# A written-out list of operations in place of a greedy scheduler, with GpSimd conversions, work in halves and means copied by engines

## The chip, the cores and the metric

The kernel runs on one core of one Trainium2 chip. The core has five engines with queues of their own, each of which works strictly in order: TensorE (PE in the rows; PEld is its weight load), VectorE (DVE), ScalarE (ACT), GpSimd (POOL) and SyncE (SP), which here only issues transfers. An instruction that needs another engine's result waits on a semaphore, and everything behind it on its engine waits too. The metric is the device time of one execution in microseconds, as the median of several runs.

## The reference

Inputs are q, k and v of 4 batches, 8 heads, 768 positions and 64 columns, and the weights of a two-layer block for the 3072 resulting tokens of 512 columns.

```python
k_sum = k.reshape(B, H, nb, block, D).max(axis=3)     # blocks of 32 keys
v_sum = v.reshape(B, H, nb, block, D).mean(axis=3)
scores_l = scale * q @ k^T, kept where |i - j| < 16
scores_s = scale * q @ k_sum^T + log(32)
a = softmax(concatenate([scores_l, scores_s]))
x = a @ concatenate([v, v_sum])
h = x @ w_in                                          # 512 -> 1024
solu = h * softmax(h)
ln = (solu - mean) / sqrt(var + 1e-6) * g_ln
out = ln @ w_out                                      # 1024 -> 512
```

## The kernel before

**Attention.** A batch has three groups `g` of 256 queries; a group has two halves `pp` of four heads. For one half, `scores` multiplies the queries with a window of 96 keys and 24 block maxima (tile `s`, 8 blocks of 128x120), VectorE adds the mask and takes the maximum (`e`, `nm`, L670), ScalarE takes the exponentials (L678), VectorE or GpSimd multiplies with the reciprocal of the sum. `values_turn` transposes (`t`, L706) into `at`, and `values` multiplies with the rows of v and the block means (`vt`; tile `x`, L753), which gives 256 tokens times 256 columns. The block means of v stand in rows 96 to 119 of `vt`. For the first group they aren't there yet, and `values` takes them from `vsum` in matmuls of its own (L745); `vsum` comes from three loads `st_v` that TensorE sums (L538). For the next two groups ScalarE's queue issues a transfer that copies `vsum` into `vt` (L614).

**Weights.** `w_in` and `w_out` come as eight loads of 512 KB each (`raw`), 64-bit numbers of which `rounded` makes 32-bit ones in five steps: the high word scaled (L446 on ScalarE, L448 on VectorE), the sign (L452), the low word's top bits (L457 on ScalarE, L459 on VectorE), a shift (L462), and an addition (L362 on VectorE, L363 on GpSimd). Each weight is then split in a rounded part and the rest (`w`), since all large products are made of three matmuls in a rounded format.

**The two layers.** `first(t)` multiplies 128 tokens with `w_in` (`h`, L905; 8 pieces of three matmuls, four for each half of 512 columns). From tile 8 on, `first_two` makes two tiles at a time with seven products in place of eight (`hu`, `hl`, `hf`, L924), from sums of weights that `sum_weights` prepares in `ws_own`. `solu` is the softmax product and the norm (L977 to L1020, tile `he`). The result is transposed, by TensorE (`lt`) for tiles 0 to 5, and from tile 6 on by a trip through memory: `send` writes `tbl` to `farl` (L1030, L1034), `fetch` reads it back as `lt` (L1040), and `rows_split` splits it into `lh` and `ll`. `second` multiplies with `w_out` (`o`, L1100), and the result is scaled on its way out of the accumulator (`os`, L1106) and stored (`out`, L1110).

**Order.** The program first makes a list of 1890 operations, each with the engines that can do it and an assumed price for each. `Plan.order` then simulates the engines and takes, again and again, the operation that can begin first, with due times breaking ties; 34 stored seeds shift the due times and the leaning to one engine at random. What comes out is the order of each engine's queue. Where the plan sees TensorE idle before 80 us, `issue` puts in fillers: matmuls with zeros (`zero`, L1292), which write to an accumulator that is free, and of which the first group needs no load.

Of the kernel before, what the change touches and what calls it, by code (L numbers as in the profile page):

```python
# [11 lines left out]
F32 = mybir.dt.float32  # L12
# [9 lines left out]
P = 128  # L22
# [17 lines left out]
LAG = 3  # L40
NHE = 4
# [5 lines left out]
FARK = 1.6  # L47
# [10 lines left out]
LATE_ROWS = 1.6  # L58
# [19 lines left out]
class Op:  # L78
    def __init__(self, can, deps, prio, nbytes, port):
        self.can, self.deps, self.engine, self.fn, self.port = can, deps, None, None, port  # L80
        self.first = next(iter(can))
        self.prio, self.nbytes, self.end, self.start, self.users, self.left = prio, nbytes, None, None, [], 0
        self.then, self.lean, self.late = None, 0.0, 0.0


class Plan:
# [7 lines left out]
    SMALL, LATE = 40.0, 50.0  # L94
    LAND = 2.2
# [3 lines left out]
    WAIT, FAR = 1.5, 200  # L99
    DEAR = {"dve": 1.0, "act": 0.3, "pool": 1.0}  # L100
    SYNC = 0.16
    NOISE = 3.0
    SHIFTS = (0.03, 8.0), (0.1, 4.0), (0.01, 25.0), (0.3, 2.0)
    SEARCHED = 310714843, 238293564, 386810029, 279445761, 931279529, 632185560, 289310670, 654992179, 446561498,\
        963011826, 180951599, 12257908, 813613886, 304267884, 394060430, 404011354, 302942999, 329802036,\
        1009020170, 829060042, 248380619, 141359939, 863688038, 95572169, 50878939, 562274274, 430477149,\
        296645202, 49801974, 349489558, 909137202, 110286346, 476818994, 599154748,
# [45 lines left out]
    def op(self, engine, cost, fn, r=(), w=(), nbytes=0, after=(), alt=(), port=False):  # L153
# [5 lines left out]
        def of(table, part):  # L159
            for k, v in table.items():  # L160
# [4 lines left out]
               len(self.ops), nbytes, port)  # L165
# [21 lines left out]
    def issue(self):  # L187

        for o in self.ops:
            o.left = len(o.deps)  # L190
            for d in o.deps:
                d.users.append(o)
        sorted_ = [o for o in self.ops if not o.left]
        for o in sorted_:
            for u in o.users:
                u.left -= 1
                if not u.left:
                    sorted_.append(u)
        for o in reversed(sorted_):
            o.due = min([u.due for u in o.users] + ([o.prio] if "pe" in o.can else []), default=o.prio)  # L200
            if "sp" in o.can:
                o.due = o.prio
        for seed in self.SEARCHED:
            self.shift(seed)
        order = self.order()
        at, done = self.START, set()
        for o in order:
            if o.engine == "pe":
                while at + self.SYNC < min(o.start + o.late, self.FILL):
                    at += self.keep_up(at, done)  # L210
                at = max(at - o.late, o.start) + o.cost * (2 if o.start < self.COLD else 1)
            done.add(o)
            o.fn()

    def shift(self, seed):


        r = random.Random(abs(seed))
        if seed < 0:
            at, wide = r.uniform(0.0, len(self.ops)), r.choice((60.0, 150.0, 400.0))  # L220
            near = [o for o in self.ops if abs(o.due - at) < wide]
            if r.random() < 0.3:
                for o in near:
                    if len(o.can) > 1 and r.random() < 0.2:
                        o.lean += r.gauss(0.0, 0.8)
                return
            share, by = r.choice(((0.03, 60.0), (0.1, 15.0), (0.3, 5.0), (0.02, 25.0)))
            for o in near:
                if r.random() < share:
                    o.due += r.gauss(0.0, by)  # L230
            return
        if seed % 5 == 4:
            for o in self.ops:
                if len(o.can) > 1 and r.random() < 0.04:
                    o.lean += r.gauss(0.0, 0.8)
            return
        share, by = self.SHIFTS[seed % 4]
        for o in self.ops:
            if r.random() < share:
                o.due += r.gauss(0.0, by)  # L240

    def order(self):

        ready, free, then, dma, held, lock = {}, {}, {}, 0.0, 0.0, 0.0
        for o in self.ops:
            o.left = len(o.deps)

        def enter(o):
            for e in o.can:
                at = max((d.end + (0.0 if d.engine == e == "pe" else self.SYNC) for d in o.deps), default=0.0)  # L250
                ready.setdefault(e, []).append((at, o))

        def begin(e, at):
            return max(free.get(e, self.START), at)

        def cost(e, o, t):
            other = lock if e == "dve" and o.port else held if e == "pool" else 0.0
            return o.can[e][0] * (2 if e == "pe" and t < self.COLD else 1) + max(other - t, 0.0)

        def loss(e, o, t):  # L260
            return cost(e, o, t) + self.DEAR.get(e, 0.0) + (o.lean if e != o.first else 0.0)

        def take(e):

            if e in then:
                return next(((begin(e, at), o) for at, o in ready[e] if o is then[e]), None)
            best = None
            for at, o in ready[e]:
                t = begin(e, at)
                if any(begin(f, at) + loss(f, o, t) < t + loss(e, o, t) for f in o.can if f != e):  # L270
                    continue
                if best is None or t < best[0] - 1e-6 or (t < best[0] + 1e-6 and (o.due, o.prio) < (best[1].due, best[1].prio)):
                    best = (t, o)
            if best is None:
                return None

            t, o = best
            for at, y in ready[e]:
                s = begin(e, at)
                if t < s and s - t < self.WAIT * (t + cost(e, o, t) - s) and y.due + self.FAR < best[1].due:  # L280
                    best = (s, y)
            return best

        for o in self.ops:
            if not o.left:
                enter(o)
        order = []
        while len(order) < len(self.ops):
            t, e, o = min(((x[0], e, x[1]) for e in ready for x in [take(e)] if x),
                          key=lambda x: (x[0], x[2].due), default=(0.0, None, None))  # L290
            if o is None:
                return None
            for f in o.can:
                ready[f] = [x for x in ready[f] if x[1] is not o]
            then.pop(e, None)
            if o.then:
                then[e] = o.then
            o.start, o.engine, (o.cost, o.fn) = t, e, o.can[e]
            o.end = free[e] = t + cost(e, o, t)
# [4 lines left out]
            if o.nbytes:  # L304
# [3 lines left out]
                o.end = (own if e == "act" else dma) + (0.2 if dma < self.LATE else self.LAND)  # L308
# [1028 lines left out]
```

## Time and profile before

| what | value |
|---|---|
| median of three runs | 364.18 us (364.12 to 364.41) |
| span of the profiled execution, first to last instruction | 362.7 us |
| TensorE busy, fillers counted | 354.6 us (98%), 3331 matmuls |
| VectorE busy | 301.2 us (83%) |
| ScalarE busy | 278.7 us (77%) |
| GpSimd busy | 157.3 us (43%) |
| transfers | 68.19 MB, mean 188 GB/s |
| granted TensorE clock | 1.000 of full speed over the span |

The median lies 1.5 us above the span: that is what an execution has around its first and last instruction. A matmul counts as busy from its start to its end, and the next one starts before that end, so 98% doesn't say that TensorE was full. Fillers count as busy as well. A better measure is the distance from one start to the next.

### The profile page before, as it was taken

The page shows a single profiled execution, that of the slowest core. Times are in us where ns is not written, and L with a number is a line of the kernel's source. Part 1 is how long each engine was busy: PE and PEld are TensorE (multiplying, and loading weights), DVE is VectorE, ACT ScalarE, POOL GpSimd, SP SyncE. Part 2 cuts the span into 40 slices and gives each one's busy share as a digit, 9 for nine tenths or more (in the row PEclk, how much of TensorE's full clock was granted, in tenths as well). Part 3 has the DMA queues.
Part 4 walks back from the last instruction along what each step waited for, and adds up shares of the span by engine and source line. Part 5 has one row for each costly group of instructions (what it writes and reads, how often), then busy time and mean ns, then how long its engine had stood idle before and what let it go on. Part 6 is the DMA issues. An engine that isn't in the chain of part 4 may idle for free.

```text
span 362.7 us, 9385 instructions
## 1 busy us (share of the span) xinstructions
PE 354.6 (98%) x3331; PEld 276.7 (76%) x3331; DVE 301.2 (83%) x967; ACT 278.7 (77%) x812; POOL 157.3 (43%) x290
## 2 busy tenths in 40 slices
PE   8899999999999999999999999899999999999996
PEld 3538767768787887788888888788888888888886
DVE  4999989997999999896998997798996987949420
ACT  4787988889769898899698697697796795855411
POOL 5413432138968974335854205209342263533100
PEclk9999999999999999999999999999999999999999
DMA  6999995337325316539399274483383183254621
GB/s 246 414 416 398 327 416 166 88 118 224 90 87 180 121 61 216 181 103 279 117 296 316 90 258 145 126 246 137 111 223 137 35 279 117 97 166 145 208 83 58
DMA packets 28530, 68.19 MB, mean 188 GB/s; under 512 B 3852, under 2 KB 13324, under 8 KB 26948
## 3 DMA queue, kind: packets, MB, share of 16 engines
q1 hardware_dynamic: 24620, 60.87, 50.0%
q10 hardware_dynamic: 3864, 6.74, 5.2%
q8 instruction: 26, 0.43, 0.5%
q14 instruction: 20, 0.16, 0.1%
HBM read 49.55 MB, written 15.73 MB: 180 GB/s over the span
## 4 chain that ended last, share of the span: by engine, by line
PE 78%; DVE 12%; DMA 7%; SPq 1%; ACT 1%; issue 1%; DVEq 0%; ACTq 0%
PE o L1100 32%; PE hu L924 11%; PE h L905 9%; PE hl L924 5%; PE x L753 5%; PE s L651 4%; PE t L706 3%; DMA st_v<-in_vr 3%; PE hf L924 3%; DVE ws_own L362 3%; DMA qt<-in_q 2%; DVE e L670 2%; PE x L1292 2%; PE vs_ps L538 1%; DMA out<-os 1%; DVE he L995 1%
## 5 line engine op out<-in xcount | busy, mean ns | idle before, releaser
L1100 PE MATMUL o<-w,lh 128*128 128x512 f32 (+1 forms) x400 | 128.8, 386 | 1.4 <-ACT os L1106 1.4
L1100 PEld LDWEIGHTS o<-w,lh 128*128 128x128 f32 x400 | 74.1, 188 | 16.7 <-ACT os L1106 1.6
L1100 PE MATMUL o<-w,ll 128*128 128x512 f32 (+1 forms) x200 | 76.2, 381 | 0.0
L678 ACT ACTIVATE e<-e,nm 128x120 f32<-128x120 f32 x192 | 73.2, 389 | 0.2 <-DVE nm L670 0.2
L905 PE MATMUL h<-w,xh 128*128 128x512 f32 x128 | 43.0, 401 | 0.0
L1100 PEld LDWEIGHTS o<-w,ll 128*128 128x128 f32 x200 | 37.6, 188 | 6.8
L670 DVE CUSTOM_DVE_ANT_0 e<-s,mask 128x120 f32<-128x120 f32 x192 | 40.6, 275 | 0.5 <-PE s L651 0.5
L678 ACT ACTIVATION_READ_ACCUMULATOR e<-e,nm 128x1 f32 x192 | 37.2, 194 | 0.0
L355 ACT COPY at<-t 120x512 f32<-120x512 f32 x42 | 22.4, 591 | 10.4 <-PE t L706 10.0
L1007 ACT ACTIVATE he<-he,nmu 128x512 f32<-128x512 f32 x31 | 21.5, 720 | 10.6 <-DVE nmu L998 10.2
L905 PEld LDWEIGHTS h<-w,xh 128*128 128x128 f32 x128 | 24.0, 188 | 6.9 <-ACT cv L446 0.8
L355 ACT CAST lh<-lt 128x512 fp32r<-128x512 f32 x38 | 21.9, 610 | 8.2 <-DMA lt<-farl 6.0
L1106 ACT ACTIVATE os<-o,y 128x512 f32<-128x512 f32 (+1 forms) x23 | 15.3, 666 | 16.3 <-PE o L1100 13.5
L753 PEld LDWEIGHTS x<-at,vt 120*64 120x64 f32 (+1 forms) x768 | 24.4, 138 | 4.5 <-issue 2.0
L357 POOL COPY kw<-ksum 128x192 f32<-128x192 f32 x22 | 9.7, 442 | 39.9 <-PE s L651 30.3
L753 PE MATMUL x<-at,vt 120*64 120x64 f32 (+1 forms) x768 | 26.6, 224 | 0.4 <-ACT at L355 0.4
L1010 ACT ACTIVATE sq<-he 128x1024 bf16<-128x1024 f32 x24 | 25.3, 1056 | 1.4 <-POOL y L1016 0.7
L1030 DVE STREAM_TRANSPOSE tbl<-he 128x1024 f32<-128x1024 f32 x18 | 22.3, 1240 | 4.5 <-DMA farl<-tbl 3.0
L905 PE MATMUL h<-w,xl 128*128 128x512 f32 x64 | 25.1, 392 | 0.0
L580 POOL TENSOR_TENSOR st_v<-st_v 96x512 f32<-96x512 f32 (+3 forms) x28 | 22.9, 826 | 4.3 <-DMA st_v<-in_vb 3.8
L987 ACT ACTIVATE he<-hs,hm 128x512 f32<-128x512 f32 x24 | 17.2, 718 | 9.2 <-DVE hm L977 9.2
L362 DVE TENSOR_TENSOR ll<-lt,lh 128x512 fp32r<-128x512 f32 x25 | 18.1, 738 | 7.2 <-ACT lh L355 7.0
(171 smaller groups left out, 840.9 us busy)
## 6 DMA issues: line engine op xcount, KB each, us to landing
vt<-in_v SPq DMA_DIRECT2D x12, 1024.0 KB
farl<-tbl SPq DMA_DIRECT2D x18, 512.0 KB
lt<-farl SPq DMA_DIRECT2D x72, 128.0 KB
kraw<-in_k SPq DMA_DIRECT2D x16, 400.0 KB
out<-os ACTq DMA_DIRECT2D x23, 256.0 KB
qt<-in_q SPq DMA_DIRECT2D x11, 512.0 KB
raw<-in_w_in SPq DMA_DIRECT2D x8, 512.0 KB
raw<-in_w_out SPq DMA_DIRECT2D x8, 512.0 KB
```

The costliest lines, as they stand in the source:

```text
L355: by = {act: lambda: nc.scalar.copy(out=to(), in_=of()), dve: lambda: nc.vector.tensor_copy(out=to(), in_=of()), pool: lambda: nc.gpsimd.t ...
L362: by = {dve: lambda: nc.vector.tensor_tensor(out=to(), in0=a(), in1=b(), op=kind), pool: lambda: nc.gpsimd.tensor_tensor(out=to(), in0=a() ...
L580: op(pool, 0.15 + w * 0.0021, lambda w=w, o=o: nc.gpsimd.tensor_tensor(out=o.ap[:n, :w], in0=x.ap[:n, :w], in1=x.ap[:n, w:2 * w], op=ALU.add),
L670: nc.vector.tensor_tensor_reduce(out=e.ap[:, n, :], in0=sc.ap[:, j, (2 * i + up) * KC:(2 * i + up + 1) * KC], in1=mask[:, mi, :], scale=-S ...
L678: nc.scalar.activation(out=e.ap[:, n, :], in_=e.ap[:, n, :], func=AF.Exp, bias=nm.ap[:, n:n + 1], scale=-1.0, accum_out=z.ap[:, n:n + 1])
L753: nc.tensor.matmul(xp()[j * D:(j + 1) * D, i, qs], vs.ap[:k, u, cs], at.ap[:k, u % 2, n[j] + u // 2, :], start=not apart, stop=not apart o ...
L905: nc.tensor.matmul(hp.ap, a.ap[:, c, ts], w.ap[:, i], start=(c == 0 and n == 0), stop=(c == NKC - 1 and n == 2))
L924: nc.tensor.matmul(to.ap, operand(y, n)[:, c], w(c).ap(i), start=first and c == 0 and k == 0, stop=c == 1 and k == 2, skip_group_check=True)
L1007: (act, 0.57, lambda sl=sl: nc.scalar.activation(out=e.ap[:, sl], in_=e.ap[:, sl], func=AF.Identity, bias=nmu.ap))], port=True)
L1010: op(act, 1.13, lambda: nc.scalar.activation(out=sq.ap, in_=e.ap, func=AF.Square, accum_out=ss.ap), r=[e], w=[sq, ss])
L1030: op(dve, 1.13, lambda: nc.vector.transpose(out=tb.ap.rearrange("p (q c a) -> p q c a", q=4, a=32), in_=of().rearrange("p (c q a) -> p q c ...
L1100: nc.tensor.matmul(o.ap[:, cols], a.ap[:, f, :], w.ap[:, i, cols], start=(f == 0 and n == 0), stop=(f == NFC - 1 and n == 2))
```

## The change

The simulation stays, but no longer decides. A table `ORDER` gives all 1890 operations in the order in which they are issued, and `OTHERS` names those that go to another engine than their first. The prices that the simulation still uses to place fillers are changed in many places; they have no effect on the work itself. The operations change too:

- `rounded` and the copies of keys may go to GpSimd. `ORDER` with `OTHERS` sends 6 of the 32 scaling steps of the weights, 8 of the 16 additions (before: 4), one of the roundings and 7 of the 22 key copies there. The same table moves the addition of the mean in `solu` (11 to 19 of 48) and the rest of `lh` (11 to 17 of 36) to GpSimd.
- For the first group, the mask, the exponentials, the division and the transposes go by halves.
- For the first group, `values` multiplies its own rows first and the means in a second operation.
- For the next two groups, engines copy the means' rows into `vt`, in four copies, in place of two transfers; for batch 1 the four small transfers of the means go from ScalarE's queue to SP's.
- `w_in` is loaded by halves of the columns, and tile 0 and tile 1 of `first` begin with the first half of the columns each, in three accumulators.

```diff
+    ORDER = [0, 1, 4, 5, 2, 7, 8, 6, 10, 55, 54, 56, 57, 12, 76, 77, 78, 79, 13, 58, 80, 9, 22, 3, 140, 21, 35, 24,
...
+    OTHERS = {
...
     def order(self):
 
-        ready, free, then, dma, held, lock = {}, {}, {}, 0.0, 0.0, 0.0
...
+        engine = {i: e for e, those in self.OTHERS.items() for i in those}
+        order = [self.ops[i] for i in self.ORDER]
+        assert len(set(order)) == len(self.ops)
+        for o in order:
+            assert o.deps <= done
+            done.add(o)
+            e = o.engine = engine.get(o.prio, o.first)
...
-    COPY_W = ((act, 0.52), (dve, 0.34))
-    COPY_K = ((act, 0.74), (dve, 0.47))
...
+    COPY_W = ((act, 0.52), (dve, 0.34), (pool, 0.7))
+    COPY_K = ((act, 0.74), (dve, 0.47), (pool, 1.05))
...
-                op0=ALU.mult))], port=True)
+                op0=ALU.mult)), (pool, 0.75, lambda: nc.gpsimd.tensor_scalar(
+                    out=high().bitcast(F32), in0=words(1).bitcast(F32), scalar1=2.0 ** -112, scalar2=0.0,
+                    op0=ALU.mult, op1=ALU.add))], port=True)
...
-            op(act, 0.34, lambda g=g: nc.scalar.dma_start(
+            op(sp, 0.75, lambda g=g: nc.sync.dma_start(
                 out=y.ap[WIN + 6 * g:WIN + 6 * g + 6, :], in_=rows.ap[32 * g:32 * g + 6, :]),
...
+        if not b:
+            for i in range(2):
+                to = lambda i=i: x.ap[WIN:KC, 2 * i:2 * i + 2]
+                of = lambda: y.ap[WIN:KC, :].rearrange("p (o c) -> p o c", o=1).broadcast_to([NB, 2, DM])
+                copy(((pool, 1.1), (dve, 0.62), (act, 0.97)), to, of, r=[y], w=[(x, 1 + i)], port=True)
+            return None
...
-        op(dve, 1.63, reduce, r=[sc], w=[e, nm])
...
+        if each:
+            for i in range(2):
+                op(dve, 0.83, lambda i=i: reduce((i,)), r=[(sc, i)], w=[(e, i), (nm, i)])
+        else:
+            op(dve, 1.63, reduce, r=[sc], w=[e, nm])
...
+        if b == g == 0:
+            for i in range(2):
+                ns = slice(4 * i, 4 * i + 4)
+                op(pe, 0.3, lambda ns=ns: turn_halves(
+                    tp.ap[:KC], lambda n: e.ap[:, n, :], range(8)[ns]), r=[(e, i)], w=[(tp, i)], kind="t")
+                copy(COPY_P, lambda ns=ns: at.ap[:KC, :, ns], lambda ns=ns: tp.ap[:KC, :, ns], r=[(tp, i)], w=[(at, i)])
...
+        if apart:
+            op(pe, 0.98, mm, r=[vs, at], w=[xb], kind="x")
+            op(pe, 0.9, means, r=[vm, at], w=[xb], kind="x")
...
-        first(t)
+        if t == 0:
+            first(0, (0,))
+            first(1, (0,))
+            first(0, (1,))
+        else:
+            first(t, (1,) if t == 1 else (0, 1))
```

Three places of the order show what moves. A row is one instruction, or several equal ones; `out<-in` are its tiles with the group and half or the batch and half in their numbers, the last number being the tile's own.

TensorE at the sums of `st_v` and the first transposes, before:

```order
L538 MATMUL vs_ps_245<-st_v_0_104,sel 24x512 x2
L538 MATMUL vs_ps_245<-st_v_1_105,sel 24x512 x2
L538 MATMUL vs_ps_245<-st_v_2_106,sel 24x512 x2
L706 MATMUL t_0_0_453<-ident,e_0_0_155 120x64 x16
L1292 LDWEIGHTS zero
L1292 MATMUL x_0_0_484<-zero 128x512
```

and now (`L1353` is the filler, `L557` the sum, `L741` the transpose):

```order
L557 MATMUL vs_ps_231<-st_v_0_104,sel 24x512 x2
L741 MATMUL t_0_0_387<-ident,e_0_0_155 120x64 x8
L557 MATMUL vs_ps_231<-st_v_1_105,sel 24x512 x2
L741 MATMUL t_0_1_409<-ident,e_0_1_156 120x64 x8
L741 MATMUL t_0_0_387<-ident,e_0_0_155 120x64 x8
L741 MATMUL t_0_1_409<-ident,e_0_1_156 120x64 x8
L1353 LDWEIGHTS zero
L1353 MATMUL x_0_0_442<-zero 128x512
```

The transposes are cut in halves and stand between the sums, where all three sums stood ahead of them.

SP's loads from the fourth load of `w_in` before:

```order
L434 DMA raw3_101<-in_w_in 128x1024
L434 DMA raw4_102<-in_w_in 128x1024
L434 DMA raw5_103<-in_w_in 128x1024
L526 DMA st_v0_0_104<-in_vr 128x1024
L526 DMA st_v0_1_105<-in_vr 128x1024
L526 DMA st_v0_2_106<-in_vr 128x1024
L608 DMA vt0_0_107<-in_v 128x2048
L434 DMA raw6_108<-in_w_in 128x1024
L434 DMA raw7_109<-in_w_in 128x1024
L602 DMA qt0_1_110<-in_q 128x1024
```

and now:

```order
L447 DMA raw1_102<-in_w_in 128x1024
L545 DMA st_v0_0_104<-in_vr 128x1024
L545 DMA st_v0_1_105<-in_vr 128x1024
L447 DMA raw6_101<-in_w_in 128x1024
L447 DMA raw4_99<-in_w_in 128x1024
L545 DMA st_v0_2_106<-in_vr 128x1024
L627 DMA vt0_0_107<-in_v 128x2048
L447 DMA raw3_103<-in_w_in 128x1024
L447 DMA raw5_108<-in_w_in 128x1024
L447 DMA raw9_125<-in_w_out 128x1024
L621 DMA qt0_1_110<-in_q 128x1024
L447 DMA raw7_109<-in_w_in 128x1024
```

`st_v` and the first half's weights (0, 2, 4, 6) come ahead of `vt0_0`, and the pieces 3, 5 and 7 behind it; one piece of `w_out` (9) comes ahead of `qt0_1`, and piece 7 behind it.

GpSimd after it has set up the masks, before:

```order
L363 TENSOR_TENSOR cv1_119<-cv1_119 128x512
L363 TENSOR_TENSOR cv0_115<-cv0_115 128x512
L357 COPY kw0_1_0_157<-ksum0_0_163 128x8x24
L363 TENSOR_TENSOR w0_323<-cv0_115,w0_323 128x512
L357 COPY kw0_1_1_158<-ksum0_1_164 128x8x24
L416 MEMSET sel_q_471 128x96
```

and now:

```order
L370 CAST w2_298<-cv2_120 128x512
L376 TENSOR_TENSOR w0_274<-cv0_115,w0_274 128x512
L376 TENSOR_TENSOR w2_298<-cv2_120,w2_298 128x512
L370 COPY kw0_1_0_157<-ksum0_0_163 128x8x24
L463 TENSOR_SCALAR cv1_119<-raw1_102 128x512
L376 TENSOR_TENSOR e0_0_0_155<-e0_0_0_155,z0_0_0_167 128x480
L429 MEMSET sel_q_453 128x96
```

A scaling step (`L463`) and a rounding (`L370 CAST`) come to GpSimd, and a half of the first division (`e0_0_0`) too.

## Rows read from the trace of the kernel before

**Rows 1.** busy time of each engine by stages, in us; columns named in its first line

```profile
core 0: us, PE busy (x) PEld busy (x) DVE busy (x) ACT busy (x) POOL busy (x), PEclk, DMA share, GB/s
10.00:32.00 22.00, 21.27 (x314) 11.64 (x314) 21.04 (x68) 17.40 (x54) 6.00 (x15) 1.00 1.03 411
32.00:60.00 28.00, 28.00 (x279) 20.14 (x276) 26.46 (x101) 24.87 (x82) 11.57 (x14) 1.00 0.97 354
60.00:82.00 22.00, 22.00 (x253) 15.47 (x252) 22.00 (x71) 19.20 (x48) 5.15 (x11) 1.00 0.32 89
...
104.00:153.50 49.50, 48.85 (x493) 38.56 (x491) 47.80 (x145) 45.51 (x135) 31.62 (x47) 1.00 0.42 143
153.50:233.00 79.50, 79.50 (x836) 65.69 (x837) 69.99 (x250) 65.25 (x199) 33.39 (x66) 1.00 0.60 192
233.00:327.00 94.00, 92.58 (x803) 76.67 (x798) 76.16 (x246) 73.13 (x214) 39.89 (x72) 1.00 0.50 156
```

**Rows 2.** the same stages, TensorE's fillers (L1292) alone

```profile
10.00:32.00 22.00, 7.13 (x29) 2.59 (x29) 1.00 1.03 411
32.00:60.00 28.00, 1.69 (x7) 0.60 (x7) 1.00 0.97 354
60.00:82.00 22.00, 4.37 (x17) 1.34 (x17) 1.00 0.32 89
```

**Rows 3.** the chain that ended last, to 36 us: start, us, what

```profile
10.03 9.76 DMA st_v<-in_vr
19.92 5.31 PE vs_ps L538 x12
31.07 0.98 PE s L651 x32
32.05 4.08 PE h L905 x17
```

**Rows 4.** timeline: start, us, engine, line, operation, tiles [idle before <-releaser]

```profile
26.15 0.43 DVE L452 TENSOR_SCALAR cv<-raw 128x512 int32<-128x512 int32 x1 [0.65 <-DMA raw<-in_w_in]
42.23 1.69 PE L1292 MATMUL x<-zero 128*128 128x512 bf16 x7
43.84 1.16 PE L753 MATMUL x<-at,vt 120*64 120x64 f32 x32
```

**Rows 5.** groups by shape, VectorE: count | busy us, mean ns | idle before

```profile
L448 DVE TENSOR_SCALAR cv<-raw 128x512 f32<-128x512 f32 x7 | 2.9, 410 | 0.0
L362 DVE CUSTOM_DVE_ANT_0 cv<-cv 128x1024 uint16<-128x1024 uint16 x12 | 8.3, 698 | 0.2 <-ACT cv L457 0.2
L362 DVE TENSOR_TENSOR ws_own<-w,w 128x512 f32<-128x512 f32 x8 | 5.9, 759 | 0.0
L362 DVE TENSOR_TENSOR ws_own<-ws_own 128x512 f32<-128x512 f32 x4 | 4.3, 1084 | 0.0
L362 DVE TENSOR_TENSOR w<-cv,w 128x512 fp32r<-128x512 f32 x6 | 4.1, 686 | 0.2
```

**Rows 6.** groups by shape, GpSimd

```profile
L363 POOL TENSOR_TENSOR cv<-cv 128x512 int32<-128x512 int32 x4 | 5.8, 1446 | 11.9 <-DVE cv L462 7.4 <-ACT cv L457 3.1 <-DVE w L362 1.4
L1003 POOL TENSOR_SCALAR he<-he,nmu 128x512 f32<-128x512 f32 x11 | 8.9, 812 | 34.7 <-DVE nmu L998 34.6
```

**Rows 7.** timeline of GpSimd, VectorE and TensorE at 234 us

```profile
233.95 1.28 POOL L363 TENSOR_TENSOR ll<-lt,lh 128x512 fp32r<-128x512 f32 x1 [2.00 <-ACT lh L355]
234.43 1.35 DVE L362 TENSOR_TENSOR ll<-lt,lh 128x512 fp32r<-128x512 f32 x1 [0.86 <-ACT lh L355]
235.77 0.50 PE L1100 MATMUL o<-w,lh 128*128 128x512 f32 x1 [1.42 <-ACT os L1106]
```

**Rows 8.** the chain again, at two switches between kinds of matmul

```profile
174.30 1.08 PE t L706 x32
175.39 1.59 PE hu L924 x6
188.50 1.36 PE hu L924 x6
```

More of the change, by code (lines that the diff above doesn't have):

```diff
@@ L151, in place, with op @@
         return b
-    def op(self, engine, cost, fn, r=(), w=(), nbytes=0, after=(), alt=(), port=False):
+    def op(self, engine, cost, fn, r=(), w=(), nbytes=0, after=(), alt=(), port=False, land=None, kind="b"):
         deps = set(after)
@@ L187, in issue @@
     def issue(self):
[L189 to L204, printed above, removed]
         order = self.order()
@@ L210, in issue @@
                     at += self.keep_up(at, done)
-                at = max(at - o.late, o.start) + o.cost * (2 if o.start < self.COLD else 1)
+                at = max(at - o.late, o.start) + o.end - o.start
             done.add(o)
             o.fn()
[L215 to L240, printed above, removed]
@@ L242, in order @@
-    def order(self):
-        ready, free, then, dma, held, lock = {}, {}, {}, 0.0, 0.0, 0.0
[L245 to L256, printed above, removed]
-            other = lock if e == "dve" and o.port else held if e == "pool" else 0.0
[L258 to L299, printed above, removed]
@@ new lines, in order @@
+    def order(self):
+        free, dma, held, lock, kind, done = {}, 0.0, 0.0, 0.0, None, set()
+        engine = {i: e for e, those in self.OTHERS.items() for i in those}
[5 more added lines that the diff above has]
+            e = o.engine = engine.get(o.prio, o.first)
+            o.cost, o.fn = o.can[e]
+            t = o.start = max([free.get(e, self.START)] + [
+                d.end + (0.0 if d.engine == e == "pe" else self.SYNC) for d in o.deps])
+            turn = self.TURN if e == "pe" and kind not in (None, o.kind) else 0.0
+            other = lock if e == "dve" and o.port else held if e == "pool" else 0.0
+            o.end = free[e] = t + (o.cost + turn) * (2 if e == "pe" and t < self.COLD else 1) + max(other - t, 0.0)
+            if e == "pe":
+                kind = o.kind
@@ L307, in order @@
                 dma += o.nbytes / next(r for t, r in self.RATES if dma <= t) * 1e-3
[L308 to L313 removed]
+                o.end = (own if e == "act" else dma) + (o.land or next(x for t, x in self.LANDS if dma <= t))
         return order
@@ L1249, in turns @@
             steps = [i for i in (t + 2, t + 3) if i < NT and i != PAIRED + 2]
-            chain([run(values_turn(*step(i)), off=0.1 if i < steps[-1] else 0.0) for i in steps])
+            chain([run(values_turn(*step(i))) for i in steps])
         behind = second_parts(t - 4 - (t > LATER))
```

207 lines of the change are left out of this document (112 added, 95 removed), and 97 rows, old and new, of tables (ORDER, OTHERS).

## The prediction

> **What bounds the kernel now.** I read four things in this order: the busy time by stages, the fillers in them, the chain of waits at the start, and the groups by shape. From 153.5 us on TensorE is the bound: it is busy for 79.50 of 79.50 us and 92.58 of 94.00 us [rows 1], at the full granted clock, with no filler, and its matmuls follow each other at 1.36 us for six, which is 0.227 us each [rows 8]. The change takes no product away: counted in the two orders, the large matmuls (600 `o`, 192 `h`, 336 of the paired tiles) and the small ones (480 transposes, 416 scores, 392 values) are as many as before. So what can be won stands in three places. The first is the start: `h` begins at 32.05 us [rows 3], and until then TensorE does fillers for much of the time (29 of them between 10 and 32 us [rows 2]). The chain there is transfers until 19.8 us, then the sums of `st_v`, transposes, values and scores [rows 3]. The second is 32 to 82 us: 24 more fillers stand there [rows 2], while VectorE is busy for 26.46 of 28 and then for 22.00 of 22.00 us [rows 1]. VectorE, not TensorE, sets the pace of that stage. The third is a few waits later on: 0.65 us between 104 and 153.5 us, and 1.42 us at 235 us [rows 1, 7].
>
> **The start.** First the rate of the loads. `st_v0_0` lands at 10.03 + 9.76 = 19.8 us [rows 3], and VectorE waits for piece 6 of `w_in` until 26.15 us [rows 4]. In SP's order these are four loads apart, 2560 KB or 2.62 MB, in 6.35 us: 413 GB/s, the same as the stage's mean of 411 [rows 1]. Now the new order. Up to and with `vt0_0` it has 7232 KB (three pieces ahead of `st_v` fewer, one half of `w_in` more behind it), where the mark at 19.8 us is 5696 KB; the 1536 KB between them take 3.8 us, so `vt0_0` lands at 23.6 us. Up to and with `qt0_1` it has 9280 KB, as many as before, so that lands at 19.8 + 3.67 MB / 0.411 = 28.7 us. In TensorE's new order the values, which took until 31.07 us before [rows 3], begin when `vt0_0` is there, since the transposes no longer stand behind 5.31 us of sums [rows 3]; they need less than 4 us, so they end at about 27.4. Six fillers follow, then the scores of the next half, which need `qt0_1`: 28.7 us. Scores take 0.98 us [rows 3], so `h` begins at 29.7 in place of 32.05: **-2.3 us**. Is VectorE ready? Up to the subtraction that the first `h` needs, its list loses 5 weight steps and two roundings, all at the 0.41 us of a weight step, two splits of 0.69 and half a division, and gains one copy, taken at 0.69 too [rows 5]: some 4 us less, so yes, unless it waits longer for the first loads. Bounds: -2.5 (the transfer of `qt0_1` is the floor) and -0.5 (VectorE late by 1.8 us).
>
> **The fillers behind it.** The new order has 16 fillers after `h` has begun, the old one 24. Seven take 43.84 - 42.23 = 1.61 us [rows 4], 0.23 us each: eight fewer are **-1.8 us**, if the wait that each covered is gone. If it is not, it comes back as idle time, so the other end is 0. I take -1.8, because the cause of these waits is VectorE's load, and that falls. Counted up to the first tile pair, VectorE loses 11 scalings of 0.41 us, 4 additions of 0.70, 4 additions on `ws_own` of about 0.9, and half a dozen single roundings and splits, in sum 15 us; it gains 12 copies, evictions and small pieces, which I put at no more than the 0.69 us of a split each, some 8 or 9 us [rows 5]. Net: **6 us off VectorE** by 140 us. They are no term of their own, since this engine is off the path from then on; they are what makes the -1.8 hold. ScalarE, busy for 19.20 of 22.0 us there [rows 1], gets five weight steps more, and three key copies, seven copies of `at`, four additions in `solu` and six DMA issues fewer; it doesn't become the bound.
>
> **What GpSimd does with it.** It takes over about 25 us until 140 us: 6 scalings at 0.81 us, 4 additions at 1.45 [rows 6], 6 or 7 more on `ws_own` and its splits at about 1.3, and copies. No row shows GpSimd copying 128x768 keys or 24x1024 means. By elements from the 512-wide operation of 0.81 us [rows 6] they would be 1.2 and 1.6 us; doubled, GpSimd would get 6 us more and would still be free for over half of 32 to 60 us, where it works 11.57 of 28 [rows 1]. I take the first value, at no cost to the path. What matters is VectorE beside it. At 234 us a split on GpSimd runs 1.28 us, and the same kind of split on VectorE, begun in the middle of it, takes 1.35 us [rows 7]; additions on `ws_own` with two inputs take 0.759 us on average in one group and 1.084 in another [rows 5]. Half of the added time lost in this way on VectorE would be 12 us, and would more than eat the 6 us. Against the 0.69 us of an undisturbed split, the twelve of them lost 4 x 0.40 + 8 x 0.07 = 2.2 us [rows 5]; with as much again for other forms I put it at 4 us for the 31.6 us that GpSimd works from 104 to 153.5 us [rows 1], an eighth. An eighth of 25 is 3 us of the 6. The Trainium skill, in "SBUF — State Buffer", section "Who interferes with whom", says that GpSimd and a VectorE instruction that has two SBUF inputs, or is in a two-port mode, exclude each other for the whole of an instruction. By that rule alone a full overlap would give all 25 us back to VectorE. The row at 234 us agrees with the rule; the mean of the stage says how seldom the two meet.
>
> **The rest.** The wait at 235 us: TensorE waits 1.42 us for `os`, which stands on ScalarE behind a split that waits for `lt`. In the new order the small transfers ahead of `lt` are spread between its pieces; this wait and the 0.65 us together can bring -2.1 at best, 0 at worst, and I take **-1.0**. Against that: the moves between small and large matmuls are 102 in place of 100, and the first six large ones behind a transpose take 0.23 us more than others [rows 8]; and at the end two half evictions now fall together. I put **+0.5** for both. The four small transfers of batch 1's means now stand in SP's queue and hold what is behind them (two key loads, a piece of `w_out`, a query load) until the means are ready; `ORDER` puts them behind `vt0_2`, which is needed first, so they cost nothing as long as those loads have over 10 us in hand. New waits from the new lists: from 0 to +4 us; the old list left about 2 us of them after 32 us, and I assume as many.
>
> Sum: -2.3 - 1.8 - 1.0 + 0.5 = -4.6 us. The profiled execution is 362.7 us of span and 1.5 us around it, 364.2, as the median; so **359.6 us**.
>
> **The rivals.**
> *GpSimd stops VectorE.* Place: 32 to 150 us, on VectorE's additions, splits and scalings in SBUF. If 40% of the 25 us are lost on it, VectorE has 10 - 6 = 4 us more than before, in a stage where it is busy 22.00 of 22.00 us, and they go to TensorE's wait. With the gain of the start: 364.2 - 2.3 + 4 = 366 us. It decides from a quarter of the time lost. For it: rows 7 and the 1.084 us. Against it: the eighth measured. By the rule named above this would be the outcome if the two engines met as often as they could.
> *The waits stay.* The fillers that are gone come back as idle time, since loads of `w_out` and queries pace 32 to 60 us (transfers at 0.97 of their share [rows 1]), and the earlier `h` is given back: 364.0.
> *All comes through.* Start -2.5, fillers -1.8, both later waits -2.1, nothing new: 357.8; with the waits of under 0.5 us also gone, 357.
> *The table changes little* would be the same as the second.
>
> **How the numbers follow.** Forecast (358.5 to 361.5) 0.48, all through 0.2, the waits stay 0.12, GpSimd stops VectorE 0.2. The range takes in the third and half of the slower case: 356.8 to 365.5. Faster by over 0.2% (0.7 us, about what a measurement of this kernel can tell from no change): 0.48 + 0.2 + 0.04 = 0.72; same 0.08; slower 0.20.
>
> **What would show it.** The first `h` before 30.2 us, and its release by the scores, which waited for `qt`; the values from about 23.7 us. No idle time on TensorE between 40 and 82 us beside the 16 fillers, and VectorE below 22.0 of 22.0 in 60 to 82 us; mean durations of `ws_own` additions and scalings on VectorE within 0.1 us of those before. If these means go up by 0.3 us and more, the first rival is right. A TensorE that is idle for more than 2 us behind 153.5 us would make the forecast wrong by the new lists themselves, which the rows of before can't show.

## The result

The changed kernel takes **358.99 us** (median of four, 358.75 to 360.69), the kernel before 364.15 us in the same session: a ratio of 0.9866 with a 95% interval of 0.9854 to 0.9878, or 5.2 us less. The prediction was 359.6 us. The profiled execution took 358.75 us, of which 357.0 us are its span (362.7 us before).

Busy time by stages of the kernel after, with the columns of [rows 1]:

```profile
10.00:32.00 22.00, 19.35 (x276) 10.46 (x273) 18.95 (x74) 19.29 (x59) 10.53 (x20) 1.00 1.03 412
32.00:60.00 28.00, 27.93 (x277) 19.81 (x277) 27.04 (x93) 27.64 (x87) 14.80 (x20) 1.00 0.62 241
60.00:82.00 22.00, 21.79 (x254) 16.85 (x256) 20.35 (x73) 18.95 (x50) 15.19 (x18) 1.00 0.64 198
...
104.00:153.50 49.50, 49.42 (x518) 40.34 (x516) 47.71 (x153) 41.18 (x126) 34.98 (x53) 1.00 0.46 144
153.50:233.00 79.50, 79.50 (x808) 66.01 (x804) 66.33 (x243) 63.28 (x194) 46.66 (x82) 1.00 0.64 205
233.00:327.00 94.00, 94.00 (x769) 77.74 (x768) 77.28 (x249) 66.81 (x202) 38.15 (x74) 1.00 0.50 162
```

The last stage is now full (92.58 of 94.00 us before). GpSimd works more in five of these six stages. VectorE falls from 22.00 to 20.35 us between 60 and 82 us, but from 32 to 60 us it is busier than before. The transfers that took 0.97 of the DMA engines there now take 0.62.

TensorE's fillers (now L1353), to be read against [rows 2]:

```profile
10.00:32.00 22.00, 4.04 (x14) 1.33 (x17) 1.00 1.03 412
32.00:60.00 28.00, 2.35 (x10) 0.89 (x12) 1.00 0.62 241
60.00:82.00 22.00, 1.30 (x4) 0.43 (x6) 1.00 0.64 198
```

The fillers behind the first `h` went from 6.06 to 3.65 us of busy time. (Some matmul records are missing; the second count, of weight loads, is nearer to what was issued.)

TensorE's waits behind 31 us, first of before, then of after: us in total, times, the longest.

```profile
PE o L1100 <- ACT os L1106: 1.4, 1, 1.4
PE x L753 <- ACT at L355: 0.4, 2, 0.2
PE hl L924 <- DVE hs L356: 0.3, 1, 0.3
```

```profile
PE x L800 <- POOL cv L476: 0.2, 1, 0.2
```

All three are gone. The chain of waits up to the first `h` of the kernel after (start, us, what):

```profile
21.75 0.79 ACT cv L472
...
22.60 0.57 issue
23.17 0.70 DVE at L369
...
28.91 1.03 PE h L1353 x4
29.94 0.98 PE s L676 x32
30.92 2.27 PE h L960 x9
```

`h` begins at 30.92 us in place of 32.05 us [rows 3]. Ahead of it stand not transfers but a weight step on ScalarE, a copy on VectorE that came late behind it, and fillers.

**Where the 5.7 us of span went.** I took each of TensorE's steps, from one matmul's start to the next one's, and set against it the undisturbed step of its kind (0.227 us for 512 columns). Behind the first `h` the two traces have equally many matmuls of each kind, fillers apart, so their undisturbed steps are the same sum, about 306.8 us. The rest of the span splits as follows:

| | before | after | difference |
|---|---|---|---|
| start of the first `h` | 32.05 | 30.92 | -1.1 |
| fillers behind it, start to start | 5.1 | 3.2 | -2.0 |
| waits and slow steps behind it | 15.4 | 12.4 | -3.0 |
| from the last matmul to the end of the span | 3.3 | 3.7 | +0.4 |

### The profile page after: what moved, and what is told of

Same layout as the page of the kernel before. It is cut to its first block, busy times and chain, and to the rows that moved or that the text cites. A ratio compares the mean times of both kernels' runs of the same rounds, so it can differ in the third digit from the quotient of the medians.

```text
span 357.0 us, 9393 instructions
## 1 busy us (share of the span) xinstructions
PE 348.5 (98%) x3305; PEld 274.9 (77%) x3311; DVE 293.2 (82%) x969; ACT 264.3 (74%) x780; POOL 189.5 (53%) x330
## 4 chain that ended last, share of the span: by engine, by line
PE 90%; DVE 5%; DMA 2%; issue 1%; ACT 1%; SPq 0%; POOL 0%; DVEq 0%
PE o L1156 37%; PE hu L980 12%; PE h L960 12%; PE x L800 6%; PE hl L980 6%; PE s L676 6%; PE t L741 3%; PE hf L980 3%; DMA kraw<-in_k 2%; DVE e L697 1%; PE vs_ps L557 1%; PE lt L741 1%; DVE ksum L537 1%; DMA out<-os 1%; PE vs_ps L570 1%
## 5 line engine op out<-in xcount | busy, mean ns | idle before, releaser
L1156 PE MATMUL o<-w,lh 128*128 128x512 f32 (+1 forms) x400 | 132.0, 386 | 0.0
L960 PE MATMUL h<-w,xh 128*128 128x512 f32 x128 | 44.1, 399 | 0.0
L376 POOL TENSOR_TENSOR ll<-lt,lh 128x512 fp32r<-128x512 f32 x17 | 22.6, 1329 | 37.6 <-ACT lh L368 21.7
L368 ACT COPY at<-t 120x512 f32<-120x512 f32 x37 | 20.2, 586 | 9.5 <-PE t L741 9.0
L1059 POOL TENSOR_SCALAR he<-he,nmu 128x512 f32<-128x512 f32 x19 | 13.5, 714 | 22.4 <-DVE nmu L1054 22.1
L368 ACT CAST lh<-lt 128x512 fp32r<-128x512 f32 x35 | 20.5, 610 | 5.9 <-PE o L1156 4.7
L1162 ACT ACTIVATE os<-o,y 128x512 f32<-128x512 f32 x17 | 11.5, 685 | 14.8 <-issue 8.0
L599 POOL TENSOR_TENSOR st_v<-st_v 96x512 f32<-96x512 f32 (+3 forms) x28 | 22.0, 789 | 0.4
L676 PE MATMUL s<-kw,qt 64*64 64x120 f32 x704 | 21.7, 267 | 0.1
```

The source lines that it names most:

```text
L368: by = {act: lambda: nc.scalar.copy(out=to(), in_=of()), dve: lambda: nc.vector.tensor_copy(out=to(), in_=of()), pool: lambda: nc.gpsimd.t ...
L376: pool: lambda: nc.gpsimd.tensor_tensor(out=to(), in0=a(), in1=b(), op=kind)}
L599: op(pool, 0.15 + w * 0.0021, lambda w=w, o=o: nc.gpsimd.tensor_tensor(out=o.ap[:n, :w], in0=x.ap[:n, :w], in1=x.ap[:n, w:2 * w], op=ALU.add),
L676: nc.tensor.matmul(sc.ap[cu * QT:(cu + 1) * QT, j, c:c + ks.shape[-1]], qs.ap[ds, 2 * pp + i, u * QT:(u + 1) * QT], ks, start=True, stop=True)
L960: nc.tensor.matmul(hp.ap, a.ap[:, c, ts], w.ap[:, i], start=(c == 0 and n == 0), stop=(c == NKC - 1 and n == 2))
L1156: nc.tensor.matmul(o.ap[:, cols], a.ap[:, f, :], w.ap[:, i, cols], start=(f == 0 and n == 0), stop=(f == NFC - 1 and n == 2))
```

## The experiments

The first question was what makes the gain: the fixed list, or the edits of the operations. The others take the terms of the sum one at a time. Times are medians; where two kernels of different sessions are compared, both stand beside a kernel before of 364.15 to 364.5 us.

### The list against the edits

`a_greedy` puts the operations of after in order by the rule of the kernel before:

```diff
-    ORDER = [0, 1, 4, 5, 2, 7, 8, 6, 10, 55, ...
+    ORDER = [ the order in which the greedy rule of before takes the same operations ]
-    OTHERS = { ... }
+    OTHERS = { the engines that this rule chose }
```

> The operations of the kernel after, with its choices of engines opened (GpSimd for conversions, halves by turns, means apart, the copies of the means' rows), but put in order by the greedy rule of the kernel before, without random shifts, in place of the fixed list. If the fixed list makes the gain, this is no faster than before: 364 us or more. If the edits of the operations make it, and the list adds little, this is at 361 us or less.

`b_unsearched` is the kernel before with that rule alone:

```diff
-        for seed in self.SEARCHED:
+        for seed in ():
```

> The kernel before with the greedy rule alone: the 34 random shifts of its due times are left out. It is what the run with the operations of after and the greedy rule has to be compared with. If the shifts were worth as much as the fixed list, it is at 368 us or more; if the greedy rule finds nearly the same order without them, it is within 1.5 us of 364.2.

Measured: 366.70 us and 365.88 us. So under one and the same rule, unsearched, the edits are worth nothing in total (0.8 us slower). The random shifts of before were worth 1.6 us (365.88 against 364.32), and the fixed list 7.7 us (366.70 against 358.99). The start is the exception. In these two kernels the first `h` begins at

```profile
31.02 0.50 PE L958 MATMUL h<-w,xh 128*128 128x512 f32 x1
```

```profile
32.29 0.50 PE L905 MATMUL h<-w,xh 128*128 128x512 f32 x1
```

(`a_greedy`, then `b_unsearched`; timeline, start first). The 1.3 us at the start come with the edits, without any list; what `a_greedy` loses, it loses behind the first `h`. Two things stay open. The rule gives GpSimd 160.9 us of work in `a_greedy` (142.5 us in `b_unsearched`), the list 189.5 us, so the list also divides the work otherwise. And no run has a list of this kind for the operations of before, so how much of the 7.7 us such a list would bring without the edits isn't shown.

### GpSimd's conversions

`a_pool_back` takes sixteen of them off GpSimd and leaves the list as it is:

```diff
-        "pool": (..., 69, ..., 186, 235, ..., 246, 264, 312, 315, 317, 319, 329, 372, 383, ..., 485, ...
+        "dve": (..., 127, 255, 256, ...    # and 186, 246, 312, 319, 383 by default; the others on ScalarE
```

> The kernel after, in its own order, with sixteen conversions up to 72 us taken off GpSimd: five scalings and three key copies of 128x768 go to ScalarE (5 x 0.67 + 3 x 0.83 = 5.8 us more there), five additions and three copies of the means' rows to VectorE (5 x 0.69 + 3 x 0.6 = 5.3 us more). Theory of the prediction: VectorE sets the pace from 32 to 82 us (busy 27.04 of 28.0 and 20.35 of 22.0 us in after), so most of the 5.3 us comes back as waits of TensorE: 361.5 to 364.5 us. Rival: what GpSimd does costs VectorE as much as it takes off it; then nothing changes, 358.3 to 360 us, and the mean of VectorE's operations with two inputs gets shorter.

Measured: 365.82 us, 6.8 us more than after, above the range of the theory. (The ten executions spread from 364.41 to 367.23 us, so the price is 5.4 us at least.) Its two stages, and its fillers in them:

```profile
32.00:60.00 28.00, 28.00 (x277) 18.91 (x276) 26.72 (x95) 27.68 (x80) 5.27 (x10) 1.00 0.58 233
60.00:82.00 22.00, 22.00 (x204) 15.48 (x202) 21.89 (x64) 19.16 (x55) 4.94 (x7) 1.00 0.58 190
```

```profile
32.00:60.00 28.00, 5.01 (x20) 1.64 (x20) 1.00 0.58 233
60.00:82.00 22.00, 4.80 (x19) 1.61 (x19) 1.00 0.58 190
```

Fillers go from 3.65 to 9.81 us, and VectorE is full again from 60 to 82 us. So this list needs GpSimd's share. Whether VectorE's five additions and three copies or ScalarE's eight conversions set the 6.8 us, the run doesn't separate: ScalarE is busy for 27.68 of 28.00 us. As the list was not searched anew, 6.8 us is the price inside this list, not of GpSimd's share in general.

`a_pool_twice` does ten of those operations, and one subtraction on GpSimd, twice:

```diff
+    TWICE = 97, 127, 235, 255, 256, 264, 315, 317, 329, 372, 485
-            o.fn()
+            for _ in range(2 if o.prio in self.TWICE else 1):
+                o.fn()
```

> The kernel after with eleven of GpSimd's conversions between 30 and 72 us done twice, one behind the other, with the same inputs and output: one subtraction, three copies of the means' rows, four scalings, three key copies, 1.28 + 3 x 1.04 + 4 x 0.80 + 3 x 0.82 = 10.1 us more on GpSimd, nothing more on VectorE. By the prediction's price (an eighth of GpSimd's time lost on VectorE) VectorE loses 1.3 us and the time rises by 0 to 1.5 us, to 359 to 360.5 us. By the first rival (VectorE stands still for 40% or more of GpSimd's time, in a stage where it is busy for 27.0 of 28 us) it rises by 4 us or more, and the means of VectorE's operations with two inputs go up; if it rises that much with those means unchanged, it is GpSimd's own results that come late.

Measured: 362.69 us, 3.7 us more. VectorE's groups between 28 and 76 us, of after and then of this kernel, where the same lines stand two further down (count | busy, mean ns):

```profile
L500 DVE SCALAR_TENSOR_TENSOR w<-cv,g_sb,w 128x512 fp32r<-128x512 f32 x8 | 5.9, 741 | 0.0
L480 DVE TENSOR_SCALAR cv<-cv 128x512 int32<-128x512 int32 x11 | 4.6, 436 | 0.0
L467 DVE TENSOR_SCALAR cv<-raw 128x512 int32<-128x512 int32 x9 | 3.7, 415 | 0.0
L375 DVE TENSOR_TENSOR e<-e,z 128x960 f32<-128x960 f32 x3 | 3.5, 1155 | 0.0
```

```profile
L502 DVE SCALAR_TENSOR_TENSOR w<-cv,g_sb,w 128x512 fp32r<-128x512 f32 x6 | 6.3, 1044 | 0.2 <-ACT w L499 0.2
L482 DVE TENSOR_SCALAR cv<-cv 128x512 int32<-128x512 int32 x11 | 6.1, 570 | 0.0
L469 DVE TENSOR_SCALAR cv<-raw 128x512 int32<-128x512 int32 x11 | 5.1, 479 | 0.0
L377 DVE TENSOR_TENSOR e<-e,z 128x960 f32<-128x960 f32 x3 | 4.1, 1361 | 0.0
```

In these four groups VectorE loses 6 x 0.303 + 11 x 0.134 + 11 x 0.064 + 3 x 0.206 = 4.6 us by the 10.1 us that were added by plan, 46%. Over the whole execution VectorE is busy for 297.5 in place of 293.2 us and GpSimd for 201.7 in place of 189.5 us, which is 4.3 by 12.2 us, 35%, since GpSimd's own instructions got longer too (copies of keys 0.823 to 0.984 us on average). Either way it is near the price of the first rival (40%) and far from the prediction's eighth, when the work stands where no plan put it. The time rose by a little less than the 4 us of that rival. TensorE's waits behind 31 us end with VectorE in four cases (2.7 us) and with a copy of GpSimd in one (0.3 us), so GpSimd's own late results are the smaller part of what these waits show.

### Are the fillers waits?

`a_no_fill` and `b_no_fill` leave out every filler behind the start:

```diff
-    COLD, FILL = 6.9, 80.0
+    COLD, FILL = 6.9, 27.0     # 29.0 in the kernel before
```

> The kernel after without the fillers that its plan puts behind the values of the first half: five ahead of the scores at 29.87 us (1.40 us in the trace of after) and thirteen behind the first h (3.2 us). Theory of the prediction: each filler covers a wait for an operand, the scores wait for the query load. Then 4.6 us of idle time stand on TensorE in their place, the scores still begin at 29.9 us, released by the load, and the time stays at 359.0 us, within 0.6. Rival: the fillers stand by the plan's own times, whether or not the operand is late. Then the scores begin at 28.5 us and the time falls by the part that was no wait, to 354.4 to 357.5 us. Third: idle time lowers the granted clock (below 0.98 in a stretch behind 27 us), and the time goes above 359.6 us.

> The kernel before without the 24 fillers behind its first h (5.1 us in its trace). Theory: they cover waits for VectorE's results; idle time of about 5 us takes their place, released by VectorE or by copies that stand behind its work, and the time stays at 364.2 us within 0.6. Rival: they stand by the plan's times; the time falls to 359.5 to 362.5 us, and the 1.8 us that the prediction put down to a lighter VectorE would be fillers that were simply not written.

Measured: 358.50 us and 362.55 us. Of after's 4.6 us of fillers 0.5 us come back, too little to be told from nothing (the intervals of the ratios, 0.9829 to 0.9882 here and 0.9854 to 0.9878 there, overlap). TensorE's timeline of `a_no_fill` at its start shows where the rest stays:

```profile
27.80 1.04 PE L787 MATMUL x<-at,vsum 120*64 120x256 f32 x8
28.86 1.05 PE L676 MATMUL s<-kw,qt 64*64 64x120 f32 x32
29.84 0.50 PE L960 MATMUL h<-w,xh 128*128 128x512 f32 x1
30.94 0.50 PE L960 MATMUL h<-w,xl 128*128 128x512 f32 x1 [0.60 <-DVE xl L813]
```

The scores follow the values at once, with no wait for the query load. Yet the second matmul of `h` stands still for the subtraction `xl` on VectorE, and what the five fillers had held is lost a microsecond later. The granted clock stays at 1.00 from 10 to 327 us.

In the kernel before 5.1 us of fillers give back 1.8 us. TensorE's waits behind 140 us in `b_no_fill` are

```profile
PE hl L924 <- DVE hs L356: 0.3, 1, 0.3
```

so the wait for `os`, 1.42 us [rows 7], is missing, although nothing was changed near it. That leaves about 0.4 us for the fillers themselves. So in both kernels nearly all of their time is lost without them too, at the operand that each covered or, as with the five, at the next one.

### The start: transposes, query load, ScalarE's list

`a_sums_first` puts TensorE's three sums ahead of the half transposes again:

```diff
-        46, 61, 52, 70, 37, 17, ... 115, 38, 114
+        46, 37, 38, 61, 52, 70, 17, ... 115, 114
```

> The kernel after with one step of its start undone: on TensorE all three sums of st_v stand ahead of the four half transposes again, instead of between them. Theory of the prediction: the transposes behind 5.3 us of sums were what held the values, so the values come about 1 to 2.5 us later than 24.3 us, the first h likewise, and the time rises to 360 to 361.5 us. Rival: weights' conversions on VectorE and ScalarE set the first h; it stays within 0.5 us of 30.85 us and the time at 359.0 us.

Measured: 362.40 us, 3.4 us more, beyond the upper end. Its timeline:

```profile
27.95 1.31 PE L800 MATMUL x<-at,vt 96*64 96x64 f32 x32
...
30.60 1.08 PE L787 MATMUL x<-at,vsum 120*64 120x256 f32 x8 [0.80 <-ACT vsum L561]
```

The values come at 27.95 us in place of 24.30. (Part of that belongs to a fall of the clock in this execution, last section, which took 364.28 us.) The transposes behind the sums hold more than the values: ScalarE stands still for the copy out of the first of them,

```profile
26.21 0.58 ACT L368 COPY at<-t 120x512 f32<-120x512 f32 x1 [5.73 <-PE t L741]
```

and the weight steps and `vsum` stand behind that copy in its list, so they are late too.

`a_qt_late` has the query load one piece later; `a_xl_first` has the rounding and the subtraction of the first half's `x` earlier. Both are without fillers behind 27 us.

```diff
-        203, 31, 44, 18, 34, ... 37, 17, 113       # a_qt_late: 18 is qt0_1, 17 piece 7 of w_in
+        203, 31, 44, 17, 18, 34, ... 37, 113
```

> The kernel after without fillers behind 27 us, and with the query load that the first large scores need one piece (512 KB, 1.25 us at 411 GB/s) later in SP's order. In the run without fillers the scores began at 28.86 us, without idle time ahead of them. If the load lands at 28.7 us in after, as the prediction had it, they now begin at about 29.9 us after 1.1 us of idle time, released by the load. If it had landed well before that, at 27.6 us or earlier, they begin at 28.9 us as before.

```diff
-        105, 106, 118, 88, 67, 94, 93, 129, 108, 190, 107, 95, 89, 128, 109, 142, 68, 96, 90, 191
+        67, 105, 106, 118, 88, 94, 93, 129, 108, 190, 89, 107, 68, 90, 95, 128, 109, 142, 96, 191
```

> The kernel after without fillers behind 27 us, and with the rounding of the first half's x on ScalarE and its subtraction on VectorE ahead of the weight step and the addition (pieces 3 and 5 of w_in) that stand before them. In the run without fillers alone, TensorE began h at 29.84 us but lost 1.1 us in its first matmuls, released by that subtraction. If the order on VectorE and ScalarE is the limit of the start, and not the query load, these 1.1 us go; if the weights then come late by as much, the loss returns within the next 24 matmuls and the time stays at 358.5 us; if not, 357.4 us.

Measured for `a_qt_late`: 358.88 us, nothing lost against 358.50 that can be told. The scores wait for the load now:

```profile
30.00 1.05 PE L676 MATMUL s<-kw,qt 64*64 64x120 f32 x32 [1.30 <-DMA qt<-in_q]
```

One piece is 1.25 us, so in after the load landed at about 28.7 us, the prediction's time. That 1.3 us of waiting cost nothing shows that the load was not what set the time.

`a_xl_first` takes 360.70 us, 2.2 us more than without the move. The stall in `h` is gone, as expected, and a larger one stands behind it. VectorE, GpSimd and TensorE in turn:

```profile
30.76 1.81 DVE L375 CUSTOM_DVE_ANT_0 cv<-cv 128x1024 uint16<-128x1024 uint16 x1
```

```profile
30.72 1.29 POOL L376 TENSOR_TENSOR cv<-cv 128x512 int32<-128x512 int32 x1 [3.41 <-ACT cv L472]
```

```profile
35.24 0.95 PE L676 MATMUL s<-kw,qt 64*64 64x120 f32 x28 [2.82 <-ACT kw L368]
```

The weight addition that I put behind the subtraction meets GpSimd's addition and takes 1.81 us instead of 0.69 us. ScalarE, whose next rounding needs it, stands still for 2.01 us, and the key copy behind that rounding holds the scores. The Trainium skill, "SBUF — State Buffer", section "Who interferes with whom", calls the port that the two engines share an exclusive lock, held for the whole instruction. This row agrees: the addition begins 0.04 us behind GpSimd's 1.29 us and is longer by 1.12 us.

### A version that is faster than both

In `a_no_fill` ScalarE is idle for 0.99 us at 21.6 us, waiting for a half transpose, with a weight step behind it. `a_cv_first` has that step first; `a_cv_fill` is the same move with all fillers left in.

```diff
-        98, 63, 99, 62, 83, 72, 19, 71, 115
+        98, 63, 99, 71, 62, 83, 72, 19, 115       # 71: weight step of piece 1, 62: copy of at
-    COLD, FILL = 6.9, 80.0
+    COLD, FILL = 6.9, 22.0                         # a_cv_first only
```

> The kernel after without fillers behind 22 us, and with one move on ScalarE: the weight step of piece 1 (unsigned low half) stands ahead of the first copy of at instead of behind it. In the run without fillers ScalarE is idle for 1.0 us at 21.6 us, waiting for that transpose, and the step that then comes late holds VectorE's addition, the next copy of at and so the values (24.60 us). If this chain of ScalarE and VectorE sets the start, the values begin at 23.9 us (behind the sums), the chain up to the first h gains 0.6 us, and the time is about 357.9 us. If something else is as late, 358.5 us as without the move.

> The same move on ScalarE in the kernel after, with all its fillers left in. If the fillers ahead of the values (0.75 us) and of the scores (1.40 us) stand by the plan's times whatever the operands do, the move brings nothing: 359.0 us within 0.5. If they only stand where the operand is late, it gains 0.6 us: 358.4 us.

Measured: 357.84 us (ratio to before 0.9825, 0.9803 to 0.9846) and 358.60 us (0.9837, 0.9822 to 0.9851). The first is as expected. For the second 0.4 us against after is too little to decide. The two differ by the fillers alone: three executions of `a_cv_first` lie between 357.69 and 357.86 us (the fourth is in the last section), all four of `a_cv_fill` between 358.49 and 358.78 us. With this move the fillers cost some 0.7 us.

`a_cv_warm` adds four fillers to `a_cv_first`, where TensorE waits for the last of the first scores:

```diff
-  op(pe, 1.1, lambda i=i: mm(i), ..., kind="s")
+  op(pe, 1.1, lambda i=i: mm(i), ..., kind="s").late = 0.9 * (pp > i)
```

> The kernel of the run with the weight step first, with four more fillers (0.9 us) ahead of the last of the first scores, where TensorE is busy for 0.43 of 1.0 us from 14 us on and idle from 15.0 to 15.6 us. In the profiled execution of that run the granted clock is 0.50 of full speed (1.2 GHz) from 16.0 to 19.3 us, and the first four sums take 2.95 us in place of 1.83 us. If the idle stretch ahead of it brings the lower level on, the granted clock stays at 1.00 in all stretches, every execution lies within 0.6 us of the median, and the median stays at 357.8 us. If the clock falls for another reason, some executions are still 1.5 us or more above the median; if the fillers are too many, the scores come late and the median goes up by up to 0.9 us.

Measured: **357.65 us**, ratio 0.9809 (0.9783 to 0.9834), six executions between 357.46 and 357.90. Its timeline:

```profile
28.65 1.05 PE L676 MATMUL s<-kw,qt 64*64 64x120 f32 x32 [0.85 <-DMA qt<-in_q]
29.64 0.50 PE L960 MATMUL h<-w,xh 128*128 128x512 f32 x1
29.97 0.42 PE L960 MATMUL h<-w,xl 128*128 128x512 f32 x1
```

Here the query load is the floor at last. The scores wait for it until 28.65 us and `h` begins at 29.64 us without a stall: the 28.7 and 29.7 us of the prediction, in a kernel in which ScalarE's list no longer stands in the way. The values begin at 23.63 us there, as the prediction had it (23.7).

## Why the prediction held, point by point

**The start, -2.3 forecast, -1.1 measured.** Two signs that the prediction named did not show: `h` came at 30.92 us, not before 30.2, and the scores ahead of it did not wait for `qt`. The rate of the loads was right: the query load landed at about 28.7 us (`a_qt_late`, `a_cv_warm`). The step that failed is "Is VectorE ready? ... so yes". I counted how much VectorE's list loses up to the first `h`, not whom it waits for. The copy of `at` on VectorE stood behind an addition, that behind a weight step on ScalarE, and that behind a copy which waited for a transpose. So the values began at 24.30 us, not 23.7, and ended 1.1 us later than the 27.4 forecast; `xl` was later still. My lower end of -0.5 had VectorE late by 1.8 us.

**The fillers, -1.8 forecast, -2.0 measured.** The size holds, and that the waits behind the fillers went with them: left out, the fillers give next to nothing back, and with GpSimd's share taken back they rise to 9.8 us. The reason holds in part. VectorE's load fell from 60 us on (20.35 of 22.0 us), but between 32 and 60 us it rose from 26.46 to 27.04 us; from 10 to 153.5 us it was busy for 133.8 in place of 136.2 us, some 2 us less where 6 were forecast. I take it that the list also shortened the chains in which VectorE, ScalarE and GpSimd wait for each other; no run shows that by itself.

**The later waits, -1.0 forecast, -3.0 measured.** This is the term that was mis-sized most. The listed waits fell from 2.1 to 0.2 us, the whole of my bound. A further 1.1 us are many steps a little shorter; I can't put them down to one cause. Nor is the reason I gave for the wait at 235 us shown (small transfers spread between the pieces of `lt`): in `b_no_fill` the wait is gone with nothing changed there.

**Switches and tail, +0.5.** The tail is 0.4 us longer. The switches can't be told apart from the 1.1 us above.

**GpSimd beside VectorE.** An eighth of GpSimd's added 25 us was to be lost on VectorE. From 10 to 153.5 us GpSimd works 17.5 us more, in the whole execution 189.5 us in place of 157.3 us, and VectorE's means fell:

```profile
L375 DVE TENSOR_TENSOR ws_own<-w,w 128x512 f32<-128x512 f32 x7 | 4.9, 707 | 0.0
L375 DVE TENSOR_TENSOR ws_own<-ws_own 128x512 f32<-128x512 f32 x2 | 1.4, 680 | 0.0
```

Against [rows 5] that is 0.707 for 0.759 us and 0.680 for 1.084 us. Over all forms that both traces have, the means of VectorE make 5.3 us less at the counts of after. GpSimd's means fell as well, its addition of the mean from 0.812 to 0.714 us. Both agree with two engines that meet less often. The copies of 128x768 keys and of the means' rows, which no row of before showed, are here:

```profile
L370 POOL COPY kw<-kraw 128x768 f32<-128x768 f32 x7 | 5.8, 823 | 2.0 <-ACT he L1043 2.0
L370 POOL COPY vt<-vsum 24x1024 f32<-24x1024 f32 x3 | 3.1, 1040 | 0.1
```

0.82 and 1.04 us, where I had estimated 1.2 and 1.6; this is a part of the 25 us that did not come.

**The rivals.** "GpSimd stops VectorE" did not happen, but its price is real: 35 to 46% in `a_pool_twice`, nearly a whole instruction in `a_xl_first`. My argument against it, that the two engines seldom meet, does not hold for every order. "The waits stay" is excluded by the table of the first section. "All comes through" (357 to 357.8 us) was nearest to what the later waits did; the start fell short of it, and `a_cv_warm` gets there.

**The sum.** -1.1 - 2.0 - 3.0 + 0.4 = -5.7 us of span, against -4.6 forecast. Two errors of opposite sign, 1.2 us too much at the start and 2.1 us too little later, left 1.1 us in the span and 0.6 us in the median. That the time came so near is in part luck.

## What to carry to other kernels

A long list and the edits that it orders have no separate prices: here the edits alone were worth nothing, the list on top of them 7.7 us, and the list without GpSimd's share was slower than the kernel before. To see whether a step will be ready, follow the order of every engine that feeds it back to a transfer; a count of the work taken off one engine says too little. Where GpSimd and VectorE work side by side, what counts is which instructions meet: 32 us more on GpSimd made VectorE's instructions no longer in one order, and 12 us more, put in without a plan, made them 4.3 us longer.

## What the hardware showed that I had not expected

The granted clock of TensorE can fall in the start, in some executions of a program and not in others. In the profiled execution of `a_cv_first`, and then in that of `a_cv_warm`, with the columns of [rows 1]:

```profile
14.00:15.00 1.00, 0.43 (x2) 0.00 (x0) 1.00 (x4) 0.97 (x7) 0.64 (x2) 1.00 1.06 422
15.00:15.50 0.50, 0.00 (x0) 0.00 (x0) 0.50 (x7) 0.50 (x4) 0.00 (x0) 1.00 0.94 385
...
16.00:19.30 3.30, 2.83 (x27) 1.10 (x20) 2.62 (x13) 3.23 (x15) 0.82 (x1) 0.50 1.04 420
```

```profile
14.00:15.00 1.00, 1.00 (x6) 0.49 (x5) 1.00 (x4) 0.97 (x7) 0.54 (x1) 1.00 1.05 418
15.00:15.50 0.50, 0.47 (x3) 0.00 (x0) 0.50 (x8) 0.50 (x5) 0.00 (x0) 1.00 0.92 377
...
16.00:19.30 3.30, 3.05 (x34) 1.15 (x29) 2.70 (x13) 3.21 (x15) 0.78 (x1) 1.00 1.04 418
```

TensorE is busy for 0.43 of the 1.5 us before 15.5 us in the first and for 1.47 in the second. From 16.0 to 19.3 us the first runs at 0.50 of full speed, 1.2 GHz, and its first four sums take 2.95 us in place of 1.83 us. That execution took 359.37 us, the three others of the kernel 357.69 to 357.86 us. With the idle stretch filled, none of six executions shows it; as it came in one of four, that is a sign and no proof. The idle stretch alone does not bring it on: in the profiled execution of after TensorE was busy for less still, 0.34 of the same 1.5 us, and the clock stayed at 1.00, from 16.0 to 19.3 us too.

```profile
14.00:15.00 1.00, 0.30 (x2) 0.00 (x0) 1.00 (x6) 0.97 (x7) 0.70 (x2) 1.00 1.07 426
15.00:15.50 0.50, 0.04 (x3) 0.04 (x3) 0.50 (x7) 0.50 (x5) 0.00 (x0) 1.00 0.94 385
```

The profiled executions of `a_sums_first` and `a_pool_twice` have such a fall too; their medians are of executions without it. The slowest execution of the changed kernel, 360.69 us, has a mean clock of 0.993; the kernel before, busy for all of the 1.5 us in its profiled execution, has executions at 0.994 and 0.995 as well (366.88, 365.11 and 367.05 us). Where the clock fell in these four no trace shows. So fillers in the start may do more than cover a wait, since an idle stretch can be followed by the lower clock; that they prevent it isn't shown.
